# Reads of all four heads in one full array, block transposes of x on VectorE, and a fixed sequence of loads

## The chip, the cores and the metric

The kernel runs on one core of a Trainium2 chip. The metric is the device time of one execution in microseconds (us); the median of three runs is 222.47 us (222.35 to 223.09). The profile is of one such execution. The engines are TensorE (PE; PEld are its weight loads), VectorE (DVE), ScalarE (ACT), GpSimd (POOL) and SyncE (SP), which here only issues DMAs.

## The reference, cut to what matters

Two blocks stand one behind the other: an attention in which 512 token rows and 32 state rows of each head read each other, and a "mixture of depths" layer that picks the 128 best rows of each batch and puts them through two dense layers.

```python
# x: (8, 8, 512, 64)   state: (8, 8, 32, 64)   batch, head, row, depth
scores = scale * x @ state^T ;  a = softmax(scores)  ; xread = a @ state      # 512 rows
scores2 = scale * state @ x^T ; a2 = softmax(scores2) ; sread = a2 @ x        # 32 rows
y = concat([xread, sread], rows)      # (8, 8, 544, 64) -> (8, 544, 512), heads side by side
s = y @ w_gate                        # one number a row
for b in range(8):
    top = the 128 rows of y[b] with the largest s
    out[b] = y[b]
    out[b, top] += sigmoid(s[top]) * (relu(y[b, top] @ w1) @ w2)              # 512 -> 1024 -> 512
```

All of it is in float32.

## The kernel before, in words

**Attention of one batch.** The 8 heads stand as two groups (g) of four (q); the 32 state rows of four heads fill 128 partitions. Loads bring x with rows of 1 KB (four tokens of one head). TensorE turns x in four pieces of four 128x128 transposes (line 340), ScalarE copies each to a tile xT (line 349; in batch 0 every other one is VectorE's, line 347). The scores (line 369) are 16 matmuls in small tiles of the array. From there two ways lead on. For the x reads, VectorE turns the scores in 32x32 blocks (line 383), takes the maximum (387), subtracts (390), ScalarE takes exp (393), VectorE sums and inverts (397 to 399), multiplies (402) and turns back (405). For the state reads, VectorE takes the maximum (411), ScalarE exp with its sum (415), TensorE turns the result (469), ScalarE copies (472), TensorE multiplies with x (485), VectorE scales (490).

**The x reads (line 447).** In chunks of 128 tokens. Each of four matmuls of a chunk has two heads in its 64 rows of the array, and on its moving side st_v, the states of the two heads on a diagonal, beside a column with state times w_gate: 129 columns. So a read gives the rows and, in the last column, a part of the row's score. ScalarE copies the rows to the tile xs (451), VectorE sums the parts of the score (455). The accumulator tile has one buffer, so a chunk waits for the copy and the sum of the one before. The rows go to the output in one store (512), the state rows in four small ones (517).

**Choice.** The state rows' scores come from a product with an accumulated sum on VectorE (537) and a matmul that adds the heads (544). All 544 scores are laid along the free axis (558 to 567), each row's wins are counted (577, 604), rows with few enough losses get a place (610, 617), and a matmul with this one-hot picks their numbers and scores (632 to 637). GpSimd gathers the chosen rows from the output in HBM (524, which therefore waits for the stores), and GpSimd, ScalarE and VectorE make the sigmoid (646 to 660).

**The two dense layers** are done for the batches 0, then 1 and 2, 3 and 4, 5 and 6, and 7: rows turned (690), first layer (707), relu (711), second layer (724), the sum on VectorE (727), rows written back by GpSimd (524).

**What sets the order.** Each piece of work is a function with an engine, a planned length, the pieces it comes after, the ring buffers that it takes and uses, and a key: its batch number plus an offset by its name (the table LATER). A planner in the kernel (carry_out) goes through planned time: the engine that can begin first takes, among the pieces ready within SOON of then, the one with the lowest key. What it writes is a fixed order for each engine; on the chip each engine goes through its order and waits where it must. Rings are sized by a count of buffers: 12 tiles xT (three batches), 5 buffers of x, of which the state has the first. The loads at the start are chained per queue in the order in which they are written: x of batch 0 in four parts on SP's and ScalarE's queues in turn, the state of batches 0 and 1 behind it on ScalarE's, x of batch 1, w_gate, x of 2, the other states, x of 3, w1 and w2 on SP's.

Of the kernel before, what the change touches and what calls it, by code (L numbers as in the profile page):

```python
# [18 lines left out]
def kernel(  # L19
# [35 lines left out]
    def pool(name, bufs, **kw):  # L55
        return ctx.enter_context(tc.tile_pool(name=name, bufs=bufs, **kw))

    N_X, N_XR = 5, 8
# [11 lines left out]
    SOON = {"PE": 0.0000, "DVE": 0.4931, "ACT": 0.0000, "POOL": 1.8045, "SP": 0.3000}  # L70

    LATER = {
        "add": -100.0000, "below": 1.9500, "exp": -0.0600, "exps": -0.7084, "fetch": 0.2600, "first": 100.0000,
        "gate": -0.5600, "gate_s": 4.8280, "heads": 0.4872, "in": -1.0433, "index": -2.8646, "load": -50.0000,
        "load_x": -2.0000, "max": 4.0896, "mult": 4.3959, "numbers": 0.2545, "off": -1.9260, "oh": -2.4538,
        "out": 3.4200, "over": -2.2366, "parts": -2.6851, "pick": 0.3200, "put": -100.0000, "read": 4.9387,
        "relu": -100.0000, "row": -4.7962, "row_kept": 4.8694, "row_s": -3.1695, "row_s_kept": -0.1742,
        "rows": 5.0000, "score_s": -3.7680, "scores": -1.0816, "second": 100.0000, "sexp": -0.1370,
        "sigmoid": 0.2238, "smax": 1.1888, "sread": 1.2957, "srows": -2.7199, "ssum": 1.4281, "state_T": 0.3300,
        "state_gates": 2.6509, "states": -1.3434, "store": 4.7700, "sub": -1.8119, "sum": -4.7918,  # L80
        "tables": -4.6345, "turn": -0.1899, "turn_a": 4.0218, "turned": 4.7352, "turned_a": -5.0000,
        "twice": -2.9080, "win": 4.2491, "xg": 90.0000, "xg_kept": -100.0000,
# [6 lines left out]
    class Ring:  # L89
# [4 lines left out]
        def take(self, buf):  # L94
            self.taken.append(buf)
            buf.ap = self.where.tile(self.shape, self.dtype, name=self.name, tag=self.name, bufs=self.bufs)

    class Piece:
        def __init__(self, engine, length, fn, after, takes, uses, key, lands):
            self.engine, self.length, self.fn, self.lands = engine, length, fn, lands  # L100
            self.name, self.key = key[1], key[0] + LATER.get(key[1], 0.0)
# [10 lines left out]
    def carry_out():  # L112
# [7 lines left out]
        while left:  # L120
# [15 lines left out]
            assert ready, "the plan cannot go on"  # L136
# [9 lines left out]
        for p in order:  # L146
            for buf in p.takes:
                buf.ring.take(buf)
            p.fn()
# [9 lines left out]
    R_XT = sbuf("xT", [128, 2, 2, 128], 12)  # L159
# [4 lines left out]
    R_XS = sbuf("xs", [128, NC, Dm], 2)  # L164
# [9 lines left out]
    R_OT = sbuf("ot", [128, Dm], 2)  # L174

# [9 lines left out]
    N_ST = 2  # L185

    def load_st(lo, hi, queue):
        queue.dma_start(out=st_c[:, lo:hi, :, 0], in_=st_src[:, lo:hi])
# [602 lines left out]
```

## Time and profile before

| | |
|---|---|
| median of the runs | 222.47 us |
| time of the profiled execution | 222.47 us |
| its span, first to last instruction | 220.7 us |
| TensorE, VectorE, ScalarE, GpSimd busy | 202.4, 124.5, 85.9, 49.9 us |
| first scores (line 369) start | 12.77 us |
| first work of the dense layers (line 707) starts | 55.50 us |
| last matmul ends | 215.4 us |
| moved by DMA | 26.59 MB in 17406 packets |

How to read it: a row of the page's engine part gives busy time and its share of the span; the slices give the same in 40 equal parts, in tenths. A group of instructions is told as line, engine, operation, output and inputs by the program's names, count, then busy time and mean in ns, then the idle time of the engine ahead of them. In the chain of work that ended last each piece has its start and its length. A row of the table by windows gives the window, its length, the busy time and count of PE, PEld, DVE, ACT and POOL, the granted clock of TensorE, the DMA engines' share and GB/s. A matmul in float32 shows as two records.

### The profile page before, as it was taken

How to read it: one execution, taken by the hardware profiler on the slowest of the kernel's cores; microseconds unless marked ns; L12 is line 12 of the kernel's file. 1: busy time of each engine (PE TensorE's matmuls, PEld its weight loads, DVE VectorE, ACT ScalarE, POOL GpSimd, SP SyncE). 2: the span in 40 equal slices, each digit the busy share in tenths (PEclk: the TensorE clock that was granted, in tenths of full speed). 3: DMA queues.
4: the chain of work that ended last, by engine and by line, in shares of the span. 5: the costliest groups of instructions: out<-in, count | busy, mean ns of one | idle time of the engine just before them, and what ended most of it. 6: DMA issues, size and time to landing. Idle time of an engine off the chain costs nothing.

```text
span 220.7 us, 4784 instructions
## 1 busy us (share of the span) xinstructions
PE 202.4 (92%) x1928; PEld 142.4 (65%) x1928; DVE 124.5 (56%) x349; ACT 85.9 (39%) x172; POOL 49.9 (23%) x128
## 2 busy tenths in 40 slices
PE   2497898898999999999999999999999999999990
PEld 2355675676878954778886455888645788447840
DVE  3159989987887897798868896730062100011001
ACT  3139878778776315453725133323301021100200
POOL 7229001041105124110142423301035200011001
PEclk9999999999999999999999999999999999999999
DMA  6999969826314301150050711502212000010001
GB/s 213 329 306 402 369 207 288 305 54 205 131 74 157 111 0 48 52 196 9 34 207 13 238 50 49 239 3 95 95 48 94 33 19 0 0 50 11 36 0 48
DMA packets 17406, 26.59 MB, mean 120 GB/s; under 512 B 5608, under 2 KB 13800, under 8 KB 16360
## 3 DMA queue, kind: packets, MB, share of 16 engines
q1 hardware_dynamic: 15032, 21.43, 28.0%
q0 software_dynamic: 1280, 4.20, 6.1%
q10 hardware_dynamic: 1072, 0.66, 0.9%
q8 instruction: 15, 0.25, 0.5%
q14 instruction: 7, 0.06, 0.1%
HBM read 15.27 MB, written 11.01 MB: 119 GB/s over the span
## 4 chain that ended last, share of the span: by engine, by line
PE 55%; issue 20%; DMA 8%; POOL 6%; ACT 5%; DVE 2%; POOLq 1%; ACTq 0%
PE ps_h L707 17%; PE ps_h L724 12%; PE ps_o L447 7%; DMA out_dram<-xs 4%; PE ps_tr L340 4%; PE ps_s L369 3%; DMA xf<-in_state_dram 3%; PE ps_tr L469 3%; PE ps_tr L485 3%; ACT a L415 2%; POOL out_dram L524 2%; PE ps_tr L604 2%; PE ps_tr L558 2%; POOL xr L524 1%; ACT xT L349 1%
## 5 line engine op out<-in xcount | busy, mean ns | idle before, releaser
L707 PE MATMUL ps_h<-xg,w 128*128 128x256 f32 (+1 forms) x320 | 60.4, 341 | 0.0
L724 PE MATMUL ps_h<-w,hT 128*128 128x512 f32 x128 | 58.9, 601 | 0.0
L707 PEld LDWEIGHTS ps_h<-xg,w 128*128 128x128 f32 x320 | 50.3, 191 | 5.9 <-issue 0.5
L724 PEld LDWEIGHTS ps_h<-w,hT 128*128 128x128 f32 x128 | 23.1, 190 | 23.2 <-issue 22.5
L340 PE MATMUL ps_tr<-ident,xf 128*128 128x128 f32 x128 | 21.5, 311 | 9.7 <-DMA xf<-in_x_dram 4.1
L727 DVE SCALAR_TENSOR_TENSOR ot<-ps_h,z,xr 128x512 f32<-128x512 f32 x8 | 6.0, 749 | 43.1 <-PE ps_h L724 43.1
L451 ACT COPY xs<-ps_o 128x512 f32<-128x512 f32 x32 | 18.8, 586 | 28.2 <-PE ps_o L447 14.1
L711 ACT ACTIVATE hT<-ps_h 128x512 f32<-128x512 f32 x16 | 9.5, 596 | 49.7 <-PE ps_h L707 49.7
L340 PEld LDWEIGHTS ps_tr<-ident,xf 128*128 128x128 f32 x128 | 15.5, 156 | 14.8 <-issue 5.3
L577 DVE SCALAR_TENSOR_TENSOR win<-srow,sc,after 128x544 bf16<-128x544 f32 (+4 forms) x40 | 18.3, 501 | 8.4 <-ACT srow L567 8.4
L447 PE MATMUL ps_o<-st_v,eT 64*128 64x129 f32 x256 | 22.9, 297 | 0.1
L447 PEld LDWEIGHTS ps_o<-st_v,eT 64*128 64x128 f32 x256 | 16.8, 186 | 6.0 <-issue 2.8
L349 ACT COPY xT<-ps_tr 128x512 f32<-128x512 f32 x30 | 16.8, 589 | 9.6 <-PE ps_tr L340 9.6
L524 POOL DMA_INDIRECT out_dram<-ot,idx x8 | 8.4, 1047 | 53.2 <-DVE ot L727 51.0
L524 POOL DMA_INDIRECT xr<-out_dram,idx x8 | 8.5, 1057 | 48.1 <-DVE idx L637 16.3
L588 POOL CAST aux<-sc 128x5 bf16<-128x5 f32 x8 | 1.9, 232 | 52.3 <-DVE sc L455 38.3
L455 DVE TENSOR_REDUCE sc<-ps_o 128x1 f32<-128x4 f32 x32 | 5.1, 158 | 12.1 <-PE ps_o L447 7.0
L415 ACT ACTIVATE a<-ps_s,nm 128x512 f32<-128x512 f32 x16 | 10.9, 689 | 2.0 <-DVE nm L411 2.0
L383 DVE STREAM_TRANSPOSE e<-ps_s 128x1024 f32<-128x1024 f32 x8 | 10.0, 1247 | 2.9 <-PE ps_s L369 2.9
L369 PE MATMUL ps_s<-xT,st_T 64*32 64x256 f32 x256 | 9.6, 413 | 1.7 <-ACT a L415 1.7
L469 PE MATMUL ps_tr<-ident,a 128*128 128x128 f32 x64 | 10.2, 284 | 1.1 <-ACT a L415 0.5
L397 DVE TENSOR_REDUCE sm<-e 128x32 f32<-128x1024 f32 x8 | 9.7, 1210 | 1.5 <-ACT e L393 1.5
(84 smaller groups left out, 229.9 us busy)
## 6 DMA issues: line engine op xcount, KB each, us to landing
out_dram<-xs SPq DMA_DIRECT2D x8, 1024.0 KB, 4.3
xf<-in_x_dram SPq DMA_DIRECT2D x14, 512.0 KB, 6.8
w<-in_moe_w_dram SPq DMA_DIRECT2D x2, 2048.0 KB, 10.1
xf<-in_x_dram SPq DMA_DIRECT2D x2, 256.0 KB, 3.2
xf<-in_x_dram ACTq DMA_DIRECT2D x2, 256.0 KB
out_dram<-xt SPq DMA_DIRECT2D x32, 16.0 KB, 2.1
xf<-in_state_dram SPq DMA_DIRECT2D x1, 384.0 KB
xf<-in_state_dram ACTq DMA_DIRECT2D x1, 128.0 KB, 7.1
```

Of the source, the lines that this page charges most:

```text
L340: nc.tensor.transpose(v[:, k, r], xf[b].ap[:, 2 * pair + k, 2 * r:2 * r + 2].rearrange("p w d -> p (w d)"), ident)
L349: nc.scalar.copy(out=t.ap, in_=v)
L369: nc.tensor.matmul(view_s()[Ns * q:Ns * (q + 1), w, g], st_T[half, b, g, Ns * q:Ns * (q + 1)], xT[2 * g + q // 2].ap[half, q % 2].rearrang ...
L383: nc.vector.transpose(out=flat(e), in_=s.ap)
L415: nc.scalar.activation(out=a.ap[:, g], in_=view_s()[:, :, g], func=AF.Exp, bias=tmp["nm"][:, g:g + 1], accum_out=tmp["ss"][:, g:g + 1])
L447: nc.tensor.matmul(view(o)[:, i, g, 0:2 * D + 1], eT.ap[half, c % 2, g, c // 2], st_v[half, b, g], start=True, stop=True)
L451: nc.scalar.copy(out=xs.ap[:, c].rearrange("p (g i m) -> p g i m", g=2, i=2), in_=view(o)[:, :, :, 0:2 * D].rearrange("p i g m -> p g i m"))
L469: nc.tensor.transpose(v[:, c], a.ap[:, g, c % 2, 128 * (c // 2):128 * (c // 2 + 1)], ident)
L524: touches(b, nc.gpsimd.indirect_dma_start(**kw), True)
L577: nc.vector.scalar_tensor_tensor(wins[c].ap[0:n], srow.ap[0:n, f:SP], sc[0:n, b, c:c + 1], after[0:n, 0:SP - f], op0=ALU.is_gt, op1=ALU.mu ...
L707: nc.tensor.matmul(v[:, f, 0:n], w1[:, j, 128 * (f0 + f):128 * (f0 + f + 1)], xg.ap[:, j, 0:n], start=(j == 0), stop=(j == ND - 1))
L724: nc.tensor.matmul(py.ap[0:m], hT.ap[:, f, lo:lo + m], w2[:, f], start=(f == 0), stop=(f == NF - 1))
```

## The change

Five things, and new numbers for the planner.

- *Reads in the full array.* st_v holds four heads on one diagonal: 4 x 64 columns and one with the gate's part. A chunk is two matmuls (one a group) with 128 rows and 257 columns instead of four with 64 and 129. xs keeps the gate's column too, and one sum on VectorE per batch takes the place of four. The store's pieces become 1 KB, as the tile xs has gaps.
- *x of batches 4 to 7.* It is loaded a second time, in pieces of 128 B, as 32x32 blocks that only need to be turned in place (eight DMAs a batch, one buffer), and VectorE turns them into xT by four block transposes. TensorE's turns and ScalarE's copies of these batches go. The ring of xT has 8 tiles instead of 12, that of gathered rows 6 instead of 8.
- *Short steps.* The one-hot is one instruction over all chunks instead of five. The state's gate product goes to GpSimd, the head sum's matmul has 128 columns, and VectorE's copy of it is a sum. Of the sigmoid's three VectorE steps two go to GpSimd. The products for the gate's column go to GpSimd as well.
- *Start.* The state of batch 0 is loaded first, twice, so that no engine has to double it; x of batch 0 comes in four parts on SP's queue alone; st_v is filled with zeros in one step; ten transposes of the identity run on TensorE before anything else.
- *Loads.* The planner gets a DMA engine of its own, with a moving time for each transfer and eight places in SP's queue; the loads of the start keep their sequence, and later loads of x stand behind them.

New in the planner, too, are all offsets in LATER and SOON, and that pieces of batch 0 get -2 where their batch number was 0 (EARLY).

```diff
-    N_X, N_XR = 5, 8
+    N_X, N_XR, N_WARM = 5, 6 if cap <= 128 else 4, 10
+    DV = 4 * D + 1
+    ON_DVE = (4, 5, 6, 7) if cap <= 128 else ()
...
+    EARLY = -2.0
...
-            self.name, self.key = key[1], key[0] + LATER.get(key[1], 0.0)
+            self.name, self.key = key[1], (key[0] or EARLY) + LATER.get(key[1], 0.0)
...
-    R_XT = sbuf("xT", [128, 2, 2, 128], 12)
+    R_XT = sbuf("xT", [128, 2, 2, 128], 8)
+    R_X2 = sbuf("x2", [128, 2, H, 4, 32], 1)
...
-    R_XS = sbuf("xs", [128, NC, Dm], 2)
+    R_XS = sbuf("xs", [128, NC, 2, 4 * D + 4], 2)
...
+    def load_x2(b, key):
+        buf = x2[b] = Buf(R_X2)
+        p_x2[b] = []
+        for w in range(2):
+            for e in range(2):
+                for r in range(2):
+                    def go(w=w, e=e, r=r):
+                        src = x[b].rearrange("h (s t r w) (e d) -> w e r t h s d", s=4, t=32, r=2, e=2)[w, e, r]
+                        o = 32 * (2 * w + e)
+                        nc.sync.dma_start(out=buf.ap[o:o + 32, r], in_=src)
...
+    p_st0 = [dma("ACT", lambda u=u: load_st(0, 1, u, nc.scalar), 0.55, 0.35, uses=[stb], key=(0, "load")) for u in range(2)]
+    p_exp0 = add("ACT", 1.5, first_exp, after=p_st0[-1].after, key=(0, "load"))
+    load_x(0, (0, "load"), 4)
+    load_x(1, (0, "load"))
+    p_wg = dma("SP", load_wg, 1.1, 0.3, key=(0, "load"))
+    p_st = dma("SP", lambda: load_st(1, B, 0, nc.sync), 0.6, 2.5, uses=[stb], key=(0, "load"), holds=4)
+    load_x(2, (0, "load"))
+    load_x(3, (0, "load"))
+    p_w1 = dma("SP", lambda: nc.sync.dma_start(out=w1, ...
+    p_zero = add("POOL", 4.3, lambda: nc.gpsimd.memset(st_v, 0.0), key=(0, "zeros"))
...
+    def warm_up():
+        for _ in range(N_WARM):
+            nc.tensor.transpose(warm.ap[:, 0:128], ident, ident)
...
+            if b in ON_DVE:
+                def turn_blocks(pair=pair, t=t):
+                    nc.vector.transpose(out=t.ap.rearrange("p k r t -> p r k t"),
+                                        in_=x2[b].ap[:, :, 2 * pair:2 * pair + 2].rearrange("p r k s d -> p r k (s d)"))
+
+                p_xT.append(add("DVE", 0.64, turn_blocks, after=p_x2[b], takes=[t], uses=[x2[b]], key=key("blocks")))
...
             def read(c=c, o=o):
                 for g in range(2):
-                    for i in range(2):
-                        half = slice(D * i, D * (i + 1))
-                        nc.tensor.matmul(view(o)[:, i, g, 0:2 * D + 1], eT.ap[half, c % 2, g, c // 2], st_v[half, b, g],
-                                         start=True, stop=True)
+                    nc.tensor.matmul(view(o)[:, g], eT.ap[:, c % 2, g, c // 2], st_v[:, b, g], start=True, stop=True)
...
-            p = add("PE", 0.66, read, after=[p_eT, p_pool[b], p_sg[b]], takes=[o], uses=[eT],
-                    key=key("read"))
-            p_sc.append(add("DVE", 0.15, gate, after=[p, p_tab], uses=[o], key=key("gate")))
+            p = add("PE", 0.46, read, after=[p_eT, p_pool[b], p_sg[b]], takes=[o], uses=[eT], key=key("read"))
...
+        def gate():
+            nc.vector.reduce_sum(out=sc[:, b, 0:NC], in_=xs.ap[:, :, :, 4 * D], axis=AX.X)
...
         def gate_state():
-            tmp["part"] = small.tile([128, 1], F32, name="part_s")
-            scr = small.tile([128, 2 * D], F32, name="scr", bufs=1)
-            nc.vector.scalar_tensor_tensor(scr, ...
+            tmp["part"] = small.tile([128, 2 * D], F32, name="part_s", bufs=2)
+            nc.gpsimd.tensor_tensor(out=tmp["part"], in0=tmp["xt"].rearrange("p g d -> p (g d)"),
+                                    in1=wg_s.rearrange("p g d -> p (g d)"), op=ALU.mult)
...
         def one_hot():
-            for c in range(NC + 1):
-                m = rows[c]
-                nc.vector.tensor_scalar(oh.ap[0:m, c], places[0:m, c], tmp["off"][0:m, c:c + 1], None, op0=ALU.is_equal)
+            nc.vector.tensor_tensor(out=oh.ap, in0=places, in1=offs[b % 2].unsqueeze(2).to_broadcast([128, NC + 1, n_slots]),
+                                    op=ALU.is_equal)
...
         if b >= 4:
             load_x(b, (b, "load_x"))
+        if b in ON_DVE:
+            load_x2(b, (b, "load_x2"))
```

## The prediction

> **What bounds the kernel now.** I read four views: the page's engine rows and slices, the table by windows, the chain that ended last, and the order of TensorE's instructions.
>
> ```profile
> PE 202.4 (92%) x1928; PEld 142.4 (65%) x1928; DVE 124.5 (56%) x349; ACT 85.9 (39%) x172; POOL 49.9 (23%) x128
> PE   2497898898999999999999999999999999999990
> DVE  3159989987887897798868896730062100011001
> ...
> L447 PE MATMUL ps_o<-st_v,eT 64*128 64x129 f32 x256 | 22.9, 297 | 0.1
> ```
>
> TensorE is the bound, with two stages. From 55 us on it never rests; VectorE works until about 165 us and then has almost nothing to do. Before 55 us the windows (busy us of PE, PEld, DVE, ACT, POOL, then clock, DMA share, GB/s) show a stage in which VectorE leads and TensorE has gaps:
>
> ```profile
> 5.00:10.00 5.00, 2.13 (x10) 1.51 (x9) 0.89 (x2) 1.17 (x2) 0.96 (x4) 1.00 1.07 323
> 15.00:20.00 5.00, 3.88 (x40) 2.93 (x46) 4.97 (x5) 4.00 (x10) 4.56 (x4) 1.00 1.06 385
> 40.00:45.00 5.00, 4.23 (x45) 3.35 (x44) 4.84 (x17) 3.50 (x8) 0.00 (x0) 1.00 0.71 262
> 100.00:110.00 10.00, 10.00 (x88) 8.21 (x86) 8.21 (x26) 5.69 (x12) 0.81 (x4) 1.00 0.02 7
> ```
>
> The order of TensorE's instructions (start, length) gives the corner points: the first scores at 12.77, the first layer work at 55.50, the last matmul's end at 208.38 + 7.03 = 215.4.
>
> ```profile
> 4.07 2.88 PE L340 MATMUL ps_tr<-ident,xf 128*128 128x128 f32 x12 [4.07 <-DMA xf<-in_x_dram]
> 12.77 1.96 PE L369 MATMUL ps_s<-xT,st_T 64*32 64x256 f32 x32
> 55.50 1.06 PE L707 MATMUL ps_h<-xg,w 128*128 128x128 f32 x8
> 59.41 1.09 PE L340 MATMUL ps_tr<-ident,xf 128*128 128x128 f32 x8
> 173.69 13.98 PE L707 MATMUL ps_h<-xg,w 128*128 128x256 f32 x64
> 208.38 7.03 PE L724 MATMUL ps_h<-w,hT 128*128 128x512 f32 x16
> ```
>
> The chain (start, length) gives the price of a read and of what stands behind it:
>
> ```profile
> 1.76 7.08 DMA xf<-in_state_dram
> 8.87 0.29 DVE xf L221
> ...
> 35.58 9.25 DMA out_dram<-xs
> 44.85 1.73 DMA out_dram<-xt
> 46.58 1.21 POOL xr L524
> ...
> 143.55 1.73 PE ps_h L707 x8
> ...
> 148.36 0.65 PE ps_o L447 x8
> 149.01 1.92 PE ps_h L707 x8
> ```
>
> So the time is: when the first scores start (12.8), plus TensorE's work after that, plus its gaps, plus a tail of 220.7 - 215.4 = 5.3. The gaps after 12.8 add up over all windows to 6.0 (5.15 of them before 55.5). The work is 215.4 - 12.8 - 6.0 = 196.6. The profiled execution's span is 220.7 and its time 222.47, which is also the median of the runs; I add these 1.8 at the end.
>
> **The change, part by part.**
>
> Turns of batches 4 to 7. 16 pieces of four transposes leave TensorE. In dense order two of them go in 1.11 (59.41 to the next piece at 60.52) and one in 0.49 (55.01 to 55.50): 16 x 0.49 = -7.8. Ends: -7.0 at 0.44 each (behind full-array work) and -9.4 at the chain's 0.59. ScalarE loses 16 copies of 0.59, 9.4 us, which is beside the path. VectorE gets 16 block transposes of 128x512: a 128x1024 one takes 1.24, so 0.64 each, +10.2.
>
> Reads. A chunk goes from four 64x129 matmuls to two of 128 rows by 257 columns. A 128x256 matmul is two records, and 64 records last 13.81 (173.69 to the next piece at 187.50): 0.216 a record. Four records of 257 columns: 0.866 against 0.65, so the read by itself gets slower. But the next full-array piece is now late by a switch: the same eight records take 1.92 behind a read and 1.73 behind a transpose, 0.19. A full-array read should not cause that. Of the 32 reads 26 have a full-array piece behind them: 26 x (0.866 - 0.84) + 6 x (0.866 - 0.65) = +2.1. Ends: +6.9 (all pay 0.216, none gives the switch back) and 0 (all give it back, and the piece ahead of a read loses a few hundredths too). I take 2.1: it follows the switch row, which is the same mix of pieces.
>
> Head sums (line 544) go from 1 column to 128: two records of 0.108 against 0.15 on the chain, say 0.25: 8 x 0.1 = +0.8. Their bounds, 0.3 to 1.2, move little.
>
> VectorE's short steps. Gates: 32 x 0.158 = 5.1 become 8 of about 0.16, -3.8, and 12.1 us of waits stood before those 32. One-hot: 9.1 becomes 8 x 0.81 (1024 elements take 1.21, so 640 some 0.81), -2.6. State gate product to GpSimd, -2.9 with its accumulator reads; state sum from a copy of 0.125 to a 128-wide reduce, +1.2; sigmoid from three steps to one, -2.5; state products and the first doubling away, -1.6. With +10.2 the sum is about -2: 122 instead of 124.5. VectorE is not relieved, its work only moves to later batches, where it has 50 us to spare at the end. GpSimd takes over 8 x 0.3 + 16 x 0.2 and some 2.5 us of products; it is idle three quarters of the span. At the start its zero fill grows from 1.9 to about 3.7 us; it and batch 0's copies must be done by the first read, at about 21, and GpSimd's state work ends at 22.0 today (17.56 + 4.45) with six more batches in it: 0.
>
> The start. Today the state's load for two batches stands behind x on ScalarE's queue and lands at 8.84; VectorE's doubling waits for it, and the copy of a turn is queued behind that: the fourth turn of batch 0 starts at 9.82 instead of 6.95. Now the state of batch 0 goes first, doubled by the transfer itself. The turns take 0.96 a piece at this stage (12 transposes in 2.88): 4.07 + 4 x 0.96 + a copy of 0.69 = 8.6 for the first scores. Ends: 7.5 (turns at warm speed; the 1 MB of x at 213 GB/s, issued from 0.7 on, allow no less) and 12.8 (nothing gained). I take 8.6, the cold speed. On the ten added transposes the row stands first: 12 transposes between 9.82 and 12.77 follow each other without a gap and still take 1.06 to 1.12 for four (0.66 later), and only behind the first scores, at 14.65, are they fast; the windows' granted clock is 1.00 throughout. The Trainium skill, "TensorE: Matmul & The Clock Gate", part "PE-mode transpose", says that transposes don't count as busy for the clock in the same way. By that rule, which speaks against this part, the warm-up is worth 0; if it did work, it would be worth 1.1 at the start and 0.8 in the scores.
>
> Gaps. This is where the turns' gain can vanish: 13 of the 16 removed pieces ran between 37 and 55 us, as work done ahead while TensorE had nothing else. If the first layers came as long after the first scores as now (42.7 us), about 6.4 us of filler would be gone and the gaps would be 6.0 + 6.6 = 12.6. But batch 0's keys are lowered by two batches, so its choice goes ahead of other batches' attention. Its own chain: scores 1, VectorE and exp 10.1, four serial reads with copies 4 x 1.65 = 6.6, rows 1.4, wins 2.95, sums to index 3.2, gather 1.05 + 3.4, turn and copy 1.1: some 31 us. In 31 us I count 25.5 of TensorE work (batch 0 whole 9.7, turns of 1 to 3 5.9, states 2.2, most of batch 1 and the scores of 2, 7.6): 5.5 of gaps, plus 2 later on (0.9 today): 7.5. Ends 5 and 17 (12.6 and 4 for loads in the way). I take 7.5, because today's first gather waited for VectorE's other batches and a store of 9.25, not for its own chain.
>
> The loads of x in blocks. 32 new DMAs of 128 KB on SP, 128 B a piece: 8192 packets a batch, 512 for each of 16 DMA engines. Ends: the ACT queue's 1072 packets took 0.9% of the engines, 31.8 us; taking the 512 of 1 KB at 44 ns (385 GB/s at full share) leaves 16 ns for one of 256 B: 8.2 us a batch; the SP queue's mean, 65.8 ns for 1.4 KB, gives 33.7. I take 8 to 10, from the smaller packets. A load runs while the batch before is worked on; scores of batches 4 to 7 are 9 to 21 us apart (14.9 in the mean), so it is hidden: 0. On SP itself a batch's eight issues take at most 8 x 1.31 (the 1536-packet state load), and a store queued behind them is that much later, with its gather. The turned x's ring goes from 12 tiles to 8, gathered rows from 8 to 6: TensorE can turn two batches ahead, not three, which is priced with the gaps; the rows of the store become pieces of 1 KB, like the loads of x: 0. The Trainium skill, "DMA: Bandwidth & Descriptors", section "Why small descriptors are slow (HBM only)", counts 3 extra cycles a packet; by it 128 B would run at 4/7, an estimate of 4.3 us a batch against 8.2 by the rows; no row shows 128 B packets.
>
> Sum: 8.6 + 196.6 - 7.8 + 2.1 + 0.8 + 7.5 + 5.3 = 213.1 span, 214.9 us.
>
> **The rivals.**
> - All comes through: start 7.5, turns -9.4, reads 0, gaps 5: 205.8 + 1.8 = 207.6. For it: the new keys put batch 0 first. Against: the cold rows.
> - The turns' work was only filler: gaps 12.6, 220.0. For it: the windows from 35 to 45, where VectorE is 95% busy. Against: the priority of batch 0.
> - The reads keep their whole price: +4.8 over the forecast, 219.7. Against: 1.92 beside 1.73.
> - Slower: block loads outlast a batch. There is one buffer, so a batch's load starts only when the one before is turned, and VectorE's queue stands still behind the first waiting block transpose, choices of earlier batches included. Batch 6's rows were turned at 167.66 and used at 173.69, a slack of 6. Two loads late by T - 14 each eat the slack and the forecast gain of 7.6 from T = 21 us a batch, 41 ns a packet; at 33.7 us batch 6 is 39 late, 33 beyond its slack, about 248. For it: 65.8 ns on this queue. Against: the ACT queue's small packets.
>
> **How the numbers follow.** Forecast (212 to 218) 0.45, all through 0.2, filler 0.15, reads 0.07, slow loads 0.13. The range, 207.5 to 222, leaves out the slow loads and a little below. What a measurement can tell from no change is 0.3%, 0.7 us: faster 0.83 (the first four cases but for the edge of the filler case), same 0.04, slower 0.13.
>
> **What would show it.** First scores at about 8.6 and, if the rule on transposes holds, still 1.9 long; first layers near 40; a read at 0.87 on the chain with 1.73 for the layers behind it; TensorE without gaps from there to about 208; no wait of VectorE for the block loads above 2 us; block loads landing within 10 us a batch. Wrong if VectorE waits for them, if gaps before the first layers exceed 10 us, or if the first layers stay at 50 or later.

## The result, and the profile after

The changed kernel is slower: 229.81 us (median of 4 runs, 229.29 to 232.67) against 222.41 us (4 runs on the same chip), a ratio of 1.035 [1.027, 1.043]. Forecast were 214.9 us, with a range of 207.5 to 222. The profiled execution is the one of 232.67 us, with a span of 230.5; it is compared below with the profiled execution of before (span 220.7). Ratios, here and below, are taken from undisturbed executions alone and medians from all, so the two can differ by up to one percent.

The page's engine rows and slices:

```profile
PE 210.2 (91%) x1746; PEld 149.1 (65%) x1746; DVE 128.5 (56%) x274; ACT 77.7 (34%) x157; POOL 64.2 (28%) x155
PE   7949959979399989999999999999999999999990
DVE  2489698793396877887997896806441100011001
PEclk9976997979859999999999999999999999999998
...
L491 PE MATMUL ps_o<-st_v,eT 128*128 128x257 f32 x128 | 35.3, 398 | 0.2 <-ACT xs L494 0.2
```

TensorE is busy for 7.8 us more than before, although 64 transposes have left it. The third row of slices is new: the granted clock, which the rows of before show at 1.00 throughout, falls several times in the first third. The table by windows (busy us of PE, PEld, DVE, ACT, POOL, then clock, DMA share, GB/s) gives the places:

```profile
15.00:20.00 5.00, 4.09 (x43) 2.42 (x41) 4.90 (x6) 3.86 (x8) 4.92 (x4) 0.50 0.99 329
35.00:40.00 5.00, 5.00 (x104) 3.82 (x89) 4.12 (x16) 1.02 (x3) 0.46 (x1) 0.69 0.50 147
60.00:70.00 10.00, 6.23 (x36) 5.91 (x37) 8.40 (x23) 1.46 (x4) 3.40 (x12) 0.66 1.04 293
```

The order of TensorE's instructions (start, length, and in brackets the idle time before and what ended it):

```profile
8.11 1.49 PE L415 MATMUL ps_s<-xT,st_T 64*32 64x256 f32 x32
...
14.47 1.97 PE L352 MATMUL ps_tr<-ident,xf 128*128 128x128 f32 x8 [2.46 <-POOL xf L229]
...
54.99 1.05 PE L754 MATMUL ps_h<-xg,w 128*128 128x128 f32 x8
...
58.72 1.05 PE L754 MATMUL ps_h<-xg,w 128*128 128x128 f32 x8
63.77 0.39 PE L671 MATMUL ps_tr<-aux,oh 128*128 128x5 bf16 x5 [4.00 <-DVE oh L655]
```

The first scores come 4.7 us earlier (8.11 against 12.77), the first layers only 0.5 (54.99 against 55.50), and two pieces into the layers TensorE stands for 4 us. The last matmul ends at 225.21, 9.8 later than before.

What VectorE was doing there, from the order of its instructions:

```profile
61.39 1.30 DVE L382 STREAM_TRANSPOSE xT<-x 128x512 f32<-128x512 f32 x2 [5.85 <-DMA x<-in_x_dram]
```

And the issues on SP's queue that lead to it (start, time until the next):

```profile
15.10 18.41 SPq L304 DMA_DIRECT2D x<-in_x_dram  x3
...
37.01 0.59 SPq L554 DMA_DIRECT2D out_dram<-xs  x1
...
52.65 0.91 SPq L304 DMA_DIRECT2D x<-in_x_dram  x1
```

VectorE waits 5.85 us at a block transpose of batch 4, the one-hot of batch 1 is queued behind it, and TensorE's gap follows. The block load that it waits for is the last of eight, which SP issued between 15.10 and 52.65; three of them together held the queue for 18.41 us (9.4, 5.5 and 3.5). The store of batch 0 is behind them: its rows were all copied at 29.42, its issue came at 37.01.

**The ledger**, by the forecast's own terms (gaps and work from the windows between the first scores and the last matmul). "Slower clock" is busy time times (1 - granted clock), summed over windows of 2.5 us up to 100 us; it is part of the work. It leaves out the slow start of both kernels, where the rows show 1.00 though TensorE is slow: the first scores of before took 1.96, the same work later 1.10.

| us | before | forecast | after |
|---|---|---|---|
| first scores start | 12.8 | 8.6 | 8.1 |
| TensorE's work after that | 196.6 | 191.7 | 203.7 |
| ... of it slower clock | 0.0 | 0 | 8.5 |
| gaps after that | 6.0 | 7.5 | 13.4 |
| tail | 5.3 | 5.3 | 5.3 |
| span | 220.7 | 213.1 | 230.5 |

Part of this belongs to the one execution, which is the slowest of its runs and 2.9 us above their median. The run warm_one below is the same kernel with nine of ten warm-up transposes left out. Its profile, of an execution of 228.73 us, has the same wait for the one-hot with less than half the length:

```profile
60.41 0.36 PE L671 MATMUL ps_tr<-aux,oh 128*128 128x5 bf16 x5 [1.62 <-DVE oh L655]
```

There VectorE waits 3.46 us for the block load, the gaps are 12.3 and the slower clock 4.4, and the scores of batch 4 start at 74.42, not at 78.36. From these scores to the last matmul's end both profiles take 146.85 us. So the ledger's 8.5 of slower clock is 4.4 in another execution, and what differs lies ahead of batch 4's scores.

### The profile page after: what moved, and what is told of

Its sections match the earlier page's. It is cut to its first block, busy times and chain, and to the rows that moved or that the text cites. A ratio compares the mean times of both kernels' runs of the same rounds, so it can differ in the third digit from the quotient of the medians.

```text
span 230.5 us, 4398 instructions
## 1 busy us (share of the span) xinstructions
PE 210.2 (91%) x1746; PEld 149.1 (65%) x1746; DVE 128.5 (56%) x274; ACT 77.7 (34%) x157; POOL 64.2 (28%) x155
## 3 DMA queue, kind: packets, MB, share of 16 engines
q1 hardware_dynamic: 56280, 26.22, 43.9%
## 4 chain that ended last, share of the span: by engine, by line
PE 58%; issue 21%; DMA 8%; ACT 5%; POOL 3%; DVE 2%; POOLq 1%; SPq 0%; DVEq 0%
PE ps_h L754 16%; PE ps_o L491 12%; PE ps_h L771 11%; PE ps_s L415 4%; PE ps_tr L511 4%; DMA x<-in_x_dram 4%; PE ps_tr L527 3%; DMA wg_s<-in_moe_w_gate_dram 3%; POOL out_dram L566 2%; PE ps_tr L644 2%; ACT a L461 2%; PE ps_tr L598 1%; DMA xf<-in_state_dram 1%; PE ps_tr L737 1%; ACT e L439 1%
## 5 line engine op out<-in xcount | busy, mean ns | idle before, releaser
L754 PEld LDWEIGHTS ps_h<-xg,w 128*128 128x128 f32 x320 | 52.5, 198 | 6.3 <-issue 1.4
L491 PE MATMUL ps_o<-st_v,eT 128*128 128x257 f32 x128 | 35.3, 398 | 0.2 <-ACT xs L494 0.2
L494 ACT COPY xs<-ps_o 128x514 f32<-128x514 f32 x32 | 18.9, 591 | 42.0 <-PE ps_o L491 42.0
L491 PEld LDWEIGHTS ps_o<-st_v,eT 128*128 128x128 f32 x128 | 22.6, 192 | 5.9 <-issue 1.9
L382 DVE STREAM_TRANSPOSE xT<-x 128x512 f32<-128x512 f32 x16 | 10.6, 690 | 6.1 <-DMA x<-in_x_dram 5.8
L511 PEld LDWEIGHTS ps_tr<-ident,a 128*128 128x128 f32 x64 | 7.8, 150 | 7.2 <-issue 2.0
L514 ACT COPY aT<-ps_tr 128x512 f32<-128x512 f32 x16 | 9.0, 590 | 9.8 <-PE ps_tr L511 9.8
L378 PE MATMUL ps_tr<-ident,xf 128*128 128x128 f32 x64 | 10.7, 306 | 0.3 <-ACT xT L395 0.2
L527 PEld LDWEIGHTS ps_tr<-xf,aT 128*32 128x32 f32 x512 | 8.3, 117 | 3.9 <-ACT aT L514 2.0
L578 POOL TENSOR_TENSOR part_s<-xt,wg_s 128x128 f32<-128x128 f32 x8 | 3.8, 480 | 24.5 <-DVE xt L532 24.5
```

What stands on the lines that cost most here:

```text
L378: nc.tensor.transpose(v[:, k, r], xf[b].ap[:, 2 * pair + k, 2 * r:2 * r + 2].rearrange("p w d -> p (w d)"), ident)
L382: nc.vector.transpose(out=t.ap.rearrange("p k r t -> p r k t"), in_=x2[b].ap[:, :, 2 * pair:2 * pair + 2].rearrange("p r k s d -> p r k (s ...
L491: nc.tensor.matmul(view(o)[:, g], eT.ap[:, c % 2, g, c // 2], st_v[:, b, g], start=True, stop=True)
L494: nc.scalar.copy(out=xs.ap[:, c, :, 0:DV], in_=view(o))
L511: nc.tensor.transpose(v[:, c], a.ap[:, g, c % 2, 128 * (c // 2):128 * (c // 2 + 1)], ident)
L527: nc.tensor.matmul(o2.ap[rr, D * g:D * (g + 1)], aT[g].ap[:, c, rr], xf[b].ap[:, 4 * g + q, c], start=(c == 0), stop=(c == NC - 1))
```

## The experiments

Ratios are to the kernel before, timed beside it on the same chip. Where the order of instructions could move by itself it is said; otherwise it is that of the kernel that was edited.

### The parts alone, in the kernel before

**The reads** (reads_alone): st_v holds four heads, a chunk is two matmuls, gathered rows have 6 buffers.

```diff
-                    for i in range(2):
-                        half = slice(D * i, D * (i + 1))
-                        nc.tensor.matmul(view(o)[:, i, g, 0:2 * D + 1], eT.ap[half, c % 2, g, c // 2], st_v[half, b, g],
-                                         start=True, stop=True)
+                    nc.tensor.matmul(view(o)[:, g, 0:4 * D + 1], eT.ap[:, c % 2, g, c // 2], st_v[:, b, g],
+                                     start=True, stop=True)
```

> The kernel before with the new reads alone (two matmuls of 128 rows by 257 columns a chunk, order of all engines kept, 6 gathered rows instead of 8). Theory 'switch': a read costs 0.866 instead of 0.65 and gives 0.19 back on the piece behind it, but is entered at 1.07 when a tiled or bf16 piece stands ahead (about half of the 32 in the changed kernel): +3 to +5 us, ratio 1.013 to 1.022, the layer piece behind a read at 1.73. Rival of the prediction: nothing given back, +6.9 us (1.031). Rival: the term as forecast, +2.1 (1.009).

228.10 us, 1.024 [1.019, 1.029]: +5.4 us, where the forecast had 2.1. Its page's engine row and its reads:

```profile
PE 209.3 (92%) x1800; PEld 149.6 (66%) x1800; DVE 124.7 (55%) x349; ACT 85.7 (38%) x172; POOL 51.1 (23%) x128
...
L447 PE MATMUL ps_o<-st_v,eT 128*128 128x257 f32 x128 | 35.3, 398 | 0.1
```

TensorE's 202.4 became 209.3 with the clock at full speed, and the reads' group 35.3 where it was 22.9. (The records of a group overlap those of its neighbours, so the group grows by more than the engine.) A read is dearer by 5.4 / 32 = 0.17 in the mean, close to the 0.216 that it takes longer by itself: little of the switch comes back. In the ledger's terms TensorE's work after the first scores grows by 6.8 (203.4), the gaps shrink by 1.6 (4.4).

**The turns** (turn_quarter): in batches 4 to 7 a turn is one transpose instead of four; ScalarE copies as much as before, from that one. The scores of these batches are therefore not the reference's.

```diff
-                for k in range(2):
-                    for r in range(2):
+                for k in range(2 if b < 4 else 1):
+                    for r in range(2 if b < 4 else 1):
...
-                    nc.scalar.copy(out=t.ap, in_=v)
+                    nc.scalar.copy(out=t.ap, in_=v if b < 4 else v[:, 0:1, 0:1].to_broadcast([128, 2, 2, 128]))
```

> The kernel before, in which a turn of batches 4 to 7 is one transpose instead of four (ScalarE copies that one four times over, so its work is the same; the scores of these batches are of wrong numbers). 16 pieces fall from 0.49 to about 0.16: 5.3 us of TensorE work less, 13 of the 16 pieces standing between 37 and 55 us. Theory 'filler': these turns ran while TensorE had nothing else, so the time stays within 1 us of before. Rival 'work' (the term of the prediction): 4 to 5.5 us faster, ratio 0.975 to 0.982.

222.41 us, 0.999 [0.995, 1.003]. Three quarters of the turns' work are gone from TensorE and nothing is faster. The window shows where they went; before, it read 4.23 busy at a clock of 1.00:

```profile
40.00:45.00 5.00, 3.39 (x28) 1.97 (x30) 4.97 (x20) 3.11 (x7) 0.00 (x0) 0.62 0.72 259
```

VectorE, the third busy column, is full at 4.97 of 5.00; TensorE has less to do and waits. Its clock falls as well, to 0.62: in the ledger's terms the work is 3.5 lower (193.1), with 4.2 of slower clock in it, the gaps 2.5 higher (8.5) and the first scores 0.8 later. What would be left of the gain at full clock this run doesn't tell.

**Block transposes on VectorE** (quarter_dve): turn_quarter, and at the scores of batches 4 to 7 four block transposes of 128x512 each, to a tile that nobody reads.

```diff
+            if b >= 4:
+                for k in range(4):
+                    nc.vector.transpose(out=spare, in_=xf[b].ap[:, 2 * k:2 * k + 2].rearrange("p h c d -> p (h c d)"))
```

> The same as the one before, with four block transposes of 128x512 added on VectorE for each of batches 4 to 7, ahead of their scores in program order, results unused: VectorE's share of the change without its loads. 16 x 0.65 = 10.4 us on VectorE. Theory 'VectorE has room': less than 1.5 us slower than the kernel with quarter turns. Rival 'VectorE leads until 100 us': 4 us or more slower than that.

231.47 us, 1.037 [1.029, 1.045]: about 9 us more than turn_quarter, for 10.4 us of VectorE work (its busy time rises from 124.5 to 134.7). Two windows of turn_quarter:

```profile
60.00:70.00 10.00, 9.78 (x187) 8.15 (x191) 8.45 (x32) 6.30 (x14) 2.83 (x6) 1.00 0.29 95
80.00:90.00 10.00, 9.20 (x87) 5.62 (x86) 7.76 (x20) 5.46 (x12) 4.30 (x9) 1.00 0.16 53
```

The same two of quarter_dve:

```profile
60.00:70.00 10.00, 7.09 (x132) 5.49 (x136) 9.34 (x25) 5.08 (x12) 0.74 (x4) 0.95 0.26 107
80.00:90.00 10.00, 8.03 (x87) 5.19 (x85) 9.83 (x30) 1.32 (x3) 2.13 (x7) 1.00 0.12 32
```

And one place in its TensorE's order:

```profile
67.56 0.71 PE L451 MATMUL ps_o<-st_v,eT 64*128 64x129 f32 x8 [2.44 <-ACT xs L455]
```

In this order of the work VectorE had no room: with it 93 to 98% busy TensorE does 2.7 and 1.2 us less in these two windows, and a read waits 2.44 us for the copy of the one before, for which ScalarE had stood 4.25 us behind a score's sum on VectorE. Over the whole kernel the gaps are 6.1 higher than in turn_quarter (14.6) and the work 4.0 (197.1), though TensorE got none; 3.6 of these are slower clock. VectorE's idle 50 us lie at the end of the kernel, and work that is due at 50 to 100 us can't use them.

**The start** (start_alone; start_full; start_hot). The state of batches 0 and 1 is loaded ahead of x instead of behind it; start_full also puts all four parts of batch 0's x on SP's queue; start_hot is start_alone with the one-hot in one instruction.

```diff
-    load_x(0, (1, "load"), 4)
     p_st0 = load("ACT", 0.6, lambda: load_st(0, N_ST, nc.scalar), uses=[stb])
     p_exp0 = add("ACT", 1.5, first_exp, after=[p_st0], key=(1, "load"))
+    load_x(0, (1, "load"), 4)
...
-                queue = nc.scalar if on == "ACT" else nc.sync
+                queue = nc.sync
```

> The kernel before with one line moved: the state of batches 0 and 1 is loaded ahead of x of batch 0 on ScalarE's queue, not behind it; every other order is kept. Theory 'an earlier start is worth something': the first scores start at 9.5 to 10.5 us instead of 12.8, VectorE starts 2 to 3 us earlier, and as VectorE leads up to 55 us the time falls by 1.5 to 3 us (ratio 0.986 to 0.993). Rival 'the head start is lost before the first layers', as in the changed kernel, where 4.7 us at the first scores were 0.5 at the first layers: within 0.7 us of before.

> The kernel with the early state load and the one-hot of the change (one instruction of 640 elements instead of five), order kept. 2.6 us of VectorE work less, 0.33 of it in batch 0's own chain. Theory: 0.3 to 1 us faster than the early load alone. Rival: the same within 0.3, since TensorE is the bound from 55 us on.

> The kernel before with the state of batches 0 and 1 loaded ahead of x (as in the run with the start alone, 221.05 us) and all four parts of batch 0's x on SP's queue instead of two on ScalarE's. With the start alone TensorE still waited 1.12 us for the last part. Theory: the last part comes earlier and the first scores start near 11, 220 to 220.5 us. Rival: the parts of one queue land one behind the other and the last is no earlier: 221 to 222.

start_alone 221.05 us, 0.992 [0.989, 0.995]; start_hot 220.80, 0.991 [0.988, 0.994], so the one-hot is worth nothing that can be told (expected for start_alone were first scores at 9.5 to 10.5; they came at 11.84); start_full 219.79 us, 0.988 [0.986, 0.990], 2.7 us below the kernel before and the best version found. TensorE's order at the start of start_alone:

```profile
8.92 1.09 PE L340 MATMUL ps_tr<-ident,xf 128*128 128x128 f32 x4 [1.12 <-DMA xf<-in_x_dram]
...
11.84 1.96 PE L369 MATMUL ps_s<-xT,st_T 64*32 64x256 f32 x32
```

And of start_full:

```profile
4.12 4.09 PE L340 MATMUL ps_tr<-ident,xf 128*128 128x128 f32 x16 [4.12 <-DMA xf<-in_x_dram]
...
9.90 1.09 PE L369 MATMUL ps_s<-xT,st_T 64*32 64x256 f32 x32
```

On one queue the parts of x come in time for four turns without a gap, and the first scores start 2.9 us earlier than before. The last matmul ends 4.3 us earlier (211.10 against 215.41) in the profiled execution, which is the fastest of its runs; by the medians 2.8 us come through.

### The changed kernel with parts undone

**The old reads** (old_reads): the four matmuls of 64 rows again; the gate's columns reach xs by a second small copy on ScalarE. **Small blocks** (blocks_small): each block transpose turns 32 columns, and ScalarE fills the tile with a constant. **Both** (blocks_small_old_reads).

```diff
+                    nc.scalar.copy(out=t.ap, in_=ident.unsqueeze(1).unsqueeze(1).to_broadcast([128, 2, 2, 128]))
-                    nc.vector.transpose(out=t.ap.rearrange("p k r t -> p r k t"),
-                                        in_=x2[b].ap[:, :, 2 * pair:2 * pair + 2].rearrange("p r k s d -> p r k (s d)"))
+                    nc.vector.transpose(out=t.ap[:, 0, 0, 0:32], in_=x2[b].ap[:, 0, 2 * pair, 0])
```

> The changed kernel with the reads of before (four matmuls of 64 rows by 129 columns; the gates' two columns are kept by a second small copy on ScalarE), order of all engines kept. Theory 'reads cost TensorE work': as the new reads alone cost 5.4 us in the kernel before, taking them out here gives 4 to 6 us back: 224 to 226 us, ratio to before 1.007 to 1.017. Rival 'gaps': in the changed kernel the start is not TensorE's, so the reads of batches 0 to 2 are free and only 20 of 32 count: 2 to 3 us back. Rival 'pairing': the new reads go with the other changes (one sum a batch) and nothing comes back: within 1 us of the changed kernel.

> The changed kernel in which each block transpose on VectorE turns only 32 columns into a corner of its tile instead of all 512 (16 of 0.69 us become 16 of about 0.1), and ScalarE, which the removed copies had left with 9.4 us more room, writes the rest of the tile with a constant; block loads, waits, places in VectorE's queue and the order of the other engines' work stay. The scores of batches 4 to 7 are then not those of the reference, and other rows are chosen. Theory: VectorE has no room from the first scores of batch 4 on, and its 9.5 us of transposes are paid nearly in full, as they were in the kernel before (8.5 to 9 for 10.4): 221 to 223 us, and the stretch from the scores of batch 4 to the end, 146.9 us in the changed kernel, shortens to about 139. Rival: the changed kernel loses its time to the late start of batch 4's scores, and VectorE then follows TensorE: 228 to 230, the stretch stays at 146 to 147.

> The kernel blocks_small with the reads of the kernel before as well (four matmuls of 64 rows and 129 columns a chunk), so that both suspected costs are out while the turns stay off TensorE. Theory: with VectorE relieved TensorE is the bound again, and the reads weigh their full 5.4 us as in the kernel before: 216 to 219 us. Rival 1: the reads keep the 2.7 to 3 us that they cost in the changed kernel: 3 below blocks_small. Rival 2 (neither was the cause, it is the late start of batch 4): 226 to 228, as with the old reads alone.

| | median, us | ratio | first scores | scores of batch 4 | last end | work | slower clock | gaps |
|---|---|---|---|---|---|---|---|---|
| after | 229.81 | 1.035 [1.027, 1.043] | 8.11 | 78.36 | 225.21 | 203.7 | 8.5 | 13.4 |
| old_reads | 227.13 | 1.021 [1.016, 1.026] | 7.83 | 75.76 | 219.75 | 197.4 | 8.4 | 14.5 |
| blocks_small | 228.71 | 1.019 [1.015, 1.023] | 8.56 | 74.76 | 222.12 | 200.7 | 4.7 | 12.8 |
| both | 223.98 | 0.996 [0.991, 1.002] | 8.25 | 68.68 | 214.02 | 195.1 | 5.5 | 10.6 |

Three things follow, from the ratios.

- With both out the loss is gone: 1.035 - 0.996 = 0.039, 8.6 us (the two intervals together leave some 2 us to either side). By the medians of all executions, which spread from 220.62 to 226.97 for the kernel with both out, it is 6.0 us, and 1.4 above the kernel before are left; the 216 to 219 us that I expected were missed either way. So reads and transposes are what made the kernel slower, and the rest of the change (start, turns off TensorE, short steps, loads, new plan) is worth -0.8 us, which can't be told from 0.
- The reads are worth 3.1 us with the transposes in place and 5.1 with them out, the transposes 3.5 with the new reads and 5.4 with the old; with intervals of some 2 us each pair may be one number (by the medians 2.6 and 4.7, 1.3 and 3.4). My expectation for blocks_small, that VectorE's transposes are paid nearly in full here too, fell: not 221 to 223 us, and the stretch from the scores of batch 4 to the end stayed, 147.4 us beside 146.9. The order made for the changed kernel runs the scores of batch 4 at 74 to 78 instead of 51 us, and from there VectorE has the room that it lacks in the order of before: 12 of the 16 transposes lie there and cost nothing that the stretch shows. What was gained lies ahead of those scores, where the other four take 2.8 us. The profiles alone don't show it: batch 4's scores start at 74.76 in blocks_small, and at 74.42 in warm_one with all transposes in place. It rests on the times.
- In blocks_small VectorE doesn't wait for a block load at all (the last was issued at 50.84 instead of 52.65); with both out it waits once, 3.58 us. How much of its 3.5 us is the transposes' own time and how much this wait, these runs don't tell.

The work column closes with known terms: 196.6 - 7.8 (turns) + 0.8 (head sums) + 5.5 (slower clock) = 195.1 with both out, which is what was measured; with the 6.8 that the reads added to TensorE's work in reads_alone and 8.5 for the clock it is 204.9 against 203.7 for the changed kernel. So the turns' 7.8 us did leave TensorE. With both out they came back as 4.6 us of gaps and 5.5 of slower clock.

**The late block loads** (block_order; block_4k). block_order puts the last five block loads of batch 4 right behind the first store and the loads of x of 5 to 7 behind them. block_4k loads as many bytes by as many DMAs in pieces of 4 KB instead of 128 B, so x of batches 4 to 7 is in the wrong order.

```diff
+        blocks = [p for p in order if p.name == "load_x2" and p.b == 4 and p.engine == "SP"]
+        late = [p for p in order[:order.index(blocks[-1])] if p.name == "load_x" and p.b >= 5 and p.engine == "SP"]
+        first = [p for p in order if p.name == "store" and p.b == 0 and p.engine == "SP"][-1]
+        moved = [p for p in blocks if order.index(p) > order.index(first)] + late
+        order = [p for p in order if p not in moved]
+        i = order.index(first) + 1
+        order[i:i] = moved
```

```diff
-                        src = x[b].rearrange("h (s t r w) (e d) -> w e r t h s d", s=4, t=32, r=2, e=2)[w, e, r]
+                        src = x[b].rearrange("h (t u) d -> h t (u d)", u=16)[4 * w + 2 * e + r]
```

> The changed kernel, with SP's queue rearranged only: the last five block loads of batch 4 stand directly behind the first store instead of being spread over 15 us, the loads of x of batches 5 to 7 behind them. Theory 'late blocks': VectorE's wait of 5.85 us for the block load of batch 4 goes to under 1, TensorE's gap of 4.0 us at 60 goes, and the low clock of 60 to 70 us with it: 5 to 7 us faster than the changed kernel (ratio to before 1.005 to 1.015). Rival 'reads': the loss is TensorE work, the gap only moves to another wait: within 1.5 us of the changed kernel.

> The changed kernel with its block loads reading pieces of 4 KB instead of 128 B, same bytes, same number of DMAs, same places in the queue; x of batches 4 to 7 then stands in the wrong order in the block tiles, so their scores are of other numbers. Theory 'small pieces': 32768 packets fewer, block loads land in under 4 us instead of 5.7, VectorE's wait for them goes to under 2 us: 4 to 7 us faster than the changed kernel. Rival 'places in the queue': SP's waits stay, since the number of DMAs stays; wait of VectorE over 4 us, less than 2 us gained.

228.81 us, 1.029 [1.023, 1.035], and 228.41 us, 1.022 [1.016, 1.028]: 1.2 us better, which can't be told from nothing, and 3.0, where 5 to 7 and 4 to 7 were expected. In block_order VectorE's 5.85 us of waiting are 1.1, but TensorE then waits a little later, for the gathered rows of batch 1:

```profile
68.13 1.08 PE L744 MATMUL ps_tr<-ident,xr 128*128 128x128 f32 x4 [2.07 <-DMA xr<-out_dram,idx]
```

The wait behind the block load hid another of half its length. In block_4k VectorE still waits 1.86 us, and the three first issues, at the same place in SP's queue, hold it for less than half as long as the 18.41 us of the small pieces:

```profile
14.09 7.70 SPq L304 DMA_DIRECT2D x<-in_x_dram  x3
```

The small packets are a cost, but not the main one.

**Clock and warm-up** (fill; warm_one). fill puts matmuls of the identity ahead of pieces that wait: 6 before the state turns of batches 1 and 2, 6 before their first turned results, 14 before the pick of batch 1. warm_one has one warm-up transpose instead of ten.

```diff
+    def fill(to, n):
+        for _ in range(n):
+            nc.tensor.matmul(to, ident, ident, start=True, stop=True)
...
+            fill(buf.ap[:, 0:128], 6 if lo == 1 else 0)
...
+                fill(v[:, 0], 6 if (b, g) in ((1, 0), (2, 0)) else 0)
...
+                fill(pa.ap[:, 128:256], 14 if b == 1 else 0)
```

```diff
-        for _ in range(N_WARM):
+        for _ in range(1):
```

> The changed kernel with identity matmuls put in front of four pieces for which TensorE waits (6 before the state turns of batches 1 and 2, 6 each before the first turn_a of batches 1 and 2, 14 before the pick of batch 1; 0.22 us each), nothing else changed. Theory 'clock': gaps over 1.5 us lower the granted clock for some 3 us afterwards, which costs about 8 us in all; filled, the clock stays at 1.00 in 15 to 20 and 60 to 70 us, and the time falls by 3 to 6 us though work is added. Rival 'gaps alone': the clock in the record costs nothing; time within 0.5 us of the changed kernel or longer.

> The changed kernel with one warm-up transpose instead of ten, nothing else changed. Theory 'transposes do not warm the clock': the first scores start at the same 8.1 us within 0.3 and the time is the same within 0.7 us. Rival 'they do': turns of batch 0 take 1.1 each instead of 0.85, first scores 0.5 to 1.2 us later and longer by 0.5, time 0 to 1.5 us longer.

fill: 230.88 us, 1.038 [1.033, 1.043]. The clock held (beside 0.50 and 0.66 without), the time did not move; the table by windows of fill:

```profile
15.00:20.00 5.00, 2.78 (x44) 1.77 (x44) 4.86 (x6) 4.20 (x10) 4.92 (x4) 1.00 1.03 374
60.00:70.00 10.00, 9.04 (x81) 8.86 (x82) 7.82 (x22) 1.46 (x4) 3.59 (x12) 1.00 0.90 239
```

The matmuls that fill are themselves in the way. Ahead of the pick of batch 1 they could start only at 60.96, when VectorE had read the sums of wins, and the pick followed them at 64.16; the one-hot was ready at 61.74, 2.4 us before. Ahead of batch 1's turned results they ran from 32.51 to 35.13, a place where in the changed kernel the turned results themselves begin (33.23). So this run does not tell what the slower clock costs. warm_one: 230.47 us, 1.038 [1.030, 1.046], first scores at 8.69, against 7.67 to 8.64 in the profiles with ten: the warm-up is worth nothing that the time can tell.

**Two runs that tell little** (turns_on_pe; early_100). The first gives the turns of batches 4 to 7 back to TensorE, the second puts batch 0 ahead of all else by its key. In both the planner makes another order for every engine.

```diff
-    ON_DVE = (4, 5, 6, 7) if cap <= 128 else ()
+    ON_DVE = ()
```

```diff
-    EARLY = -2.0
+    EARLY = -100.0
```

> The changed kernel with all turns of x on TensorE and no block loads (the list of batches for VectorE is empty; the planner makes its order anew). Theory 'block loads cost the start': TensorE gets 7.8 us of work back, VectorE loses 10.6, SP 32 DMAs; VectorE's wait of 5.85 and TensorE's gaps after 30 us go, since turns fill them: 224 to 228 us, up to 5 us faster than the changed kernel. Rival 'turns were worth their work': TensorE bound, 7.8 us slower than the changed kernel, 236 to 238.

> The changed kernel with batch 0's keys lowered by 100 instead of 2, so that every ready piece of batch 0 goes ahead of other batches in the plan (order made anew). Theory 'batch 0 was not first': its wins and picks stood behind batch 1's reads and VectorE's work; now the first layers start at 45 to 50 us instead of 55, and the time falls by 2 to 6 us. Rival 'its own chain': first layers stay within 2 us of 55, time within 2 us of the changed kernel.

235.34 us, 1.059 [1.053, 1.065], with the first layers only at 75.5: a new order, no test of the turns. 238.07 us, 1.072 [1.063, 1.080]: with the highest priority batch 0's pick came at 43.94 and its first layers at 54.2, hardly elsewhere than in the changed kernel (42.66 and 54.99), and later stages starved. So the key was not what kept the first layers at 55.

## Why the prediction was wrong

- **Turns, -7.8: wrong in what it was worth.** The step that failed first is to take 7.8 us of removed work for 7.8 us of time. The rival "the turns' work was only filler" held: removing three quarters of it in the kernel before gave 0.999. I had its evidence (13 of 16 pieces ran between 37 and 55 us, VectorE 95% busy) and gave it 0.15, on the strength of batch 0's new key.
- **VectorE, "50 us to spare": wrong.** The sum was off too, 128.5 instead of 122: block transposes 0.69 each, not 0.64, and short steps whose means overlap in the profile, so that taking them away saves less (a gate's mean is 0.158 us, but the next step starts 0.08 after it). The greater error was to set a spare that lies behind 165 us against work due at 50 to 100: 10.4 us of transposes cost 9 in the order of before, and 3.5 to 5.4 in the changed one (by the medians 1.3 to 3.4), where the forecast had nothing. "An engine at 85 to 90% in the stretch in question" should have stood as a slower rival of its own; it did not.
- **Reads, +2.1: mis-sized, 5.4** in the kernel before. The mechanism was right in its details: on the chain a read takes 0.87 behind a full-array piece, as forecast, and the layers behind it 1.73:

```profile
97.66 0.87 PE ps_o L491 x4
98.53 1.73 PE ps_h L754 x8
...
101.91 1.06 PE ps_o L491 x4
```

  But a read behind a piece in small tiles or bf16 (the last line, behind the sums of wins) takes 1.06: the switch is then paid on the read's own side, and the saving of 0.19 that I credited to 26 of 32 reads mostly moved instead of going. 5.4 lies between my forecast and my upper end of 6.9; as TensorE's work alone, 6.8, it is the upper end.
- **First layers near 40: wrong, 54.99.** The head start was lost step by step: the last read of batch 0 was copied 6.1 us earlier than before (29.42 against 35.56), its wins were counted 3.9 earlier (VectorE did batch 1's steps first), the pick 2.1 earlier (42.66 against 44.79; batch 1's reads went first on TensorE), the first layers 0.5. I had counted batch 0's own chain and not what stands between its links; that a lower key changes nothing (early_100) says that those links are not a matter of priority alone.
- **Gaps, 7.5: measured 13.4**, near the 12.6 that I gave as the "filler" case. Some 1 us of it belongs to the profiled execution (12.3 in warm_one). My place for a wait on the block loads was right (VectorE's queue stands still, the choice of an earlier batch behind it), the mechanism was another: no load outlasts a batch (a block load lands 5.7 us after its issue in the median, and VectorE waits for them this once), but the first batch's eight were issued too late, on a queue in which three issues took 18.41 us. My count of a packet was close: the added 41248 packets, 32768 of them of 128 B, took 15.3 ns each in the mean (43.9% of 16 engines' 230.5 us against 28.0% of 220.7), against 16 forecast. "On SP at most 1.31 an issue" was wrong by a factor of nearly five.
- **Clock: not in the sum**, 8.5 us of TensorE's work in the profiled execution, 4.4 in warm_one; what it costs in time stays open. I had taken full speed from the windows of before, which have no such stretches.
- **Start: right in the time, not in its rule.** 8.1 against 8.6 (range 7.5 to 12.8), and the warm-up worth nothing that can be told. But the first scores took 1.49, not 1.9, and those of start_full 1.09 with nothing but transposes ahead of them: that transposes do not speed up TensorE, by which the forecast set the warm-up at 0, does not hold in these traces. The clock's rows, 1.00 throughout, could not have told.
- **Small slips, without weight.** The reads' sum, 26 x (0.866 - 0.84) + 6 x (0.866 - 0.65), is 2.0, the filler case's gaps 6.0 + 6.4 = 12.4, and the one-hots' row is 8.5, not 9.1.

## What to carry to other kernels

Before crediting work taken off the busiest engine, ask which engine ended the waits around the removed pieces: filler that runs while TensorE waits for VectorE is worth nothing, as in turn_quarter. Spare time counts only where it lies, so set an engine's new work against its windows at the time when that work is due, not against its total. A change of five parts is best priced one by one: here a simple form of one of them, the loads of the start (start_full, -1.2%), beats the whole, and two cost more than the others bring.

## What the runs showed of the hardware that I had not expected

- The granted clock can fall after short gaps. In the changed kernel TensorE ran only transposes from about 9.6 to 18.46 us, with gaps of 2.46 and 0.69 in them, and the window from 15 to 20 shows 0.50; with six matmuls of the identity ahead of the state turns it shows 1.00. The Trainium skill, "TensorE: Matmul & The Clock Gate", "Why this matters for your kernels", sets the harmful gap at about 3 us; here a gap of 1.59 before 33.23, again with transposes on both sides, was followed by 0.69. It is not so every time: in block_4k a gap of 1.56 before 48.45, between transposes too, was followed by 1.00.
- Transposes without gaps bring TensorE to its full pace. In old_reads nothing but transposes ran before 7.83 us, and yet eight of them take 1.15 at 5.80, as eight do later (1.09):

```profile
5.80 1.15 PE L378 MATMUL ps_tr<-ident,xf 128*128 128x128 f32 x8
```

  The same page, part "PE-mode transpose", says that transposes don't count as busy in the same way; this trace does not agree, nor does start_full with its first scores of 1.09.
- A read in the full array is not free of the switch between small tiles and the full array: 0.87 behind a full-array piece, 1.06 behind another.
- Many small DMAs hold up SP's queue far beyond their own issue: three block loads of 128 KB in 128 B pieces, whose issue began at 15.10, kept it for 18.41 us, with the DMA engines full (share 0.99 from 15 to 20). With the same bytes in 4 KB pieces it was 7.70 (block_4k), so most of it is the small pieces; where the rest comes from was not tried.
